# Retention attention and a low-rank mixer MLP on one core: the order of the start-up transfers, of the first batch's chunks, and of the work beside the first MLP

## The chip, the core and the metric

The kernel runs on one core of one Trainium2 chip. The metric is the device time of one execution in microseconds (us); a median of several executions stands for a kernel. The engines are PE (matmul; PEld is its weight load), DVE (vector), ACT (scalar), POOL (GpSimd) and SP (which only issues transfers). DMA engines move data between memory and the chip; a transfer is issued by SP, ACT or POOL, in the order of that engine's own program.

## The reference

Eight batches of 576 positions, 8 heads of 64. The attention is a decayed causal product without softmax, its output is the input x of a mixer along positions (rank 32), and that feeds an MLP of 512 to 2048 to 512:

```python
scores = scale * q @ k.T                      # per batch and head, 576 x 576
ret = scores * Dmat                           # Dmat[i, j] = gamma_h ** (i - j) for i >= j, else 0
x = (ret @ v)                                 # all heads side by side: 8 x 576 x 512
u = x + ((x.T @ U) @ V).T                     # U 576 x 32, V 32 x 576
out = u + relu(u @ w_ch1) @ w_ch2             # w_ch1 512 x 2048, w_ch2 2048 x 512, float32
```

## The kernel before

**Tiling.** Positions go in chunks of 128. Two batches p share one odd chunk: an even batch has four full chunks and the first half (64 rows) of chunk XC, an odd batch has the other half of XC and four more. A batch g is `Front(g)` and then `Mlp(g)`. Front computes the attention chunk by chunk in a recurrent form, and the mixer; Mlp is a phase Y1 (`u @ w_ch1`, relu; 16 feature blocks f) and a phase Y2 (`@ w_ch2`, 16 matmuls over f for each chunk of output).

**Front, per chunk c.** `TK` transposes k (for the first two batches on PE through a PSUM tile of the pool ps_big, which has three buffers; for later ones by a DMA that SP issues), `TQ` the queries, `TX` the q and k of chunk XC. `ST` (L425) adds k-times-v to a running state and ACT copies it out (L430). `SC` makes the scores (L446), then the product of the queries with the state of the chunk before, into tile po (L462), and DVE masks the scores (L471). `RV` multiplies the masked scores with v (L483), and DVE scales the result into x (L491). `MA` and `MH` are the mixer (L512, L529; DVE adds x at L535), `MT` (L548) transposes u into uT, the input of Y1 (L647). po and the scores' tile have one buffer each, so a chunk waits for DVE's reading of the chunk before.

**Loads and casts.** `load_q` (L253), `load_kv` (L284) and `load_x` (L305) are issued by SP as float32 into staging tiles: one buffer for q, four for k and v, one for x. `cast_q` and `cast_kv` turn them into bfloat16: DVE casts q and k, POOL scales v (`scale_v`, L274). `load_mixer` (L192 to L197) brings U and V in small pieces, six transfers for part 0 and five for part 1, on SP's queue. `load_w1` (L229) and `load_w2` (L239) are four transfers each, issued by POOL, which cast to bfloat16 on the way.

**The order.** It is all written out by hand (`tc.manual_schedule`): each engine runs its instructions strictly in the order in which the Python code emits them. A list of (time, function) pairs, sorted by time, lays Front's items between those of the MLP; the times are planned costs in ns, not waits. At the start:

- SP issues q and chunk 0 of batch 0, part 0 of the mixer, chunks 1 to 3, x, part 1 of the mixer.
- `early_consts` makes the decay tables (16 small DVE multiplications at L166, two ACT exponentials) and `first_front` runs batch 0's attention in the order 0, 1, 2, 3, XC, with 28 dummy matmuls (L697) between.
- POOL issues all of w1 ahead of chunk XC's work and, by the insertion after the fourth Y1 item, all of w2. Nothing is ahead of w2 in POOL's queue that has to wait, so its four transfers leave right behind w1's.
- `load_q(1)`, and with it the rest of batch 1 behind it in SP's queue, waits for the third w1 transfer (`return dmas[-2]`). `load_q(2)` waits for the last w2 transfer.
- `interleave(y1, fill, 0.75, 1.8)` lays the mixer's end of batch 0 and all of `Front(1)` beside and behind Y1 of batch 0; Y2 of batch 0 follows when Front(1) is over, three chunks abreast and then the fourth.
- From batch 1 on the list of timed events runs: Front(2) from 0.1 of Mlp(1), each later Front(g) up to 0.65 of Mlp(g-1).

```python
i = load_q(1)
tc.add_manual_dep(i.ins, w1_last.ins.name, SYNC)
...
y1.insert(4, (0, lambda: w2_last.append(load_w2())))
interleave(y1, fill, LEAD[0], LEAD[1])
lo2 = loads_of(2)
i = lo2.pop(0)[0]()
tc.add_manual_dep(i.ins, w2_last[0].ins.name, SYNC)
for f in range(NF):
    for i in range(3):
        mlp.Y2(i, f, 1)
```

Of the kernel before, what the change touches and what calls it, by code (L numbers as in the profile page):

```python
# [41 lines left out]
def kernel(  # L42
# [37 lines left out]
    LEAD = (0.75, 1.8)  # L80
# [40 lines left out]
    lnb = consts.tile([P, 1], FP32, name="lnb")  # L121
    U_A = consts.tile([P, 5, P], BF16, name="U_A")
# [19 lines left out]
    def early_consts():  # L142
        make_identity(nc, ident)
        nc.gpsimd.memset(lnb, math.log(scale))


        for t in (posk, posq):
            iota(t[:, XC, :], [[0, H]], 4 * P, 1)
            iota(t[HALF:P, XC, :], [[0, H]], -HALF, 1)
        iota(posk[:, 0:4, :], [[P, 4], [0, H]], 0, 1)  # L150
        iota(posk[:, 5:9, :], [[P, 4], [0, H]], 0, 1)
        for j in range(J):
            r = slice(j * PJ, (j + 1) * PJ)
# [10 lines left out]
        for h in range(H):  # L164
            for t in (posk, posq):
                nc.vector.tensor_scalar(  # L166
                    out=t[:, :, h], in0=t[:, :, h], scalar1=lng[h], scalar2=None,
                    op0=ALU.mult,
                )
# [3 lines left out]
    def clear_a():  # L173
        nc.vector.memset(ret_xa[HALF:P], 0.0)
# [13 lines left out]
    def load_mixer(par):  # L188
        f, t0, m0 = ((U_fA, 0, 0), (U_fB, HALF, 1))[par]
        src = moe_U[t0:t0 + 4 * P, :].rearrange("(m p j) r -> j p m r", p=PJ, j=J)  # L190
        for j in range(J):
            nc.sync.dma_start(out=f[j * PJ:(j + 1) * PJ, m0:m0 + 4, :], in_=src[j])  # L192
        if par == 0:
            nc.sync.dma_start(out=U_fA[0:HALF, 4, :], in_=moe_U[4 * P:S, :])
            nc.sync.dma_start(out=V_nat, in_=moe_V)
        else:
            nc.sync.dma_start(out=U_fB[HALF:P, 0, :], in_=moe_U[0:HALF, :])  # L197
# [26 lines left out]
    def load_w1():  # L224
        dmas = []
        for fb in range(dff // W1B):
            cols = slice(fb * W1B, (fb + 1) * W1B)
            dmas.append(
                nc.gpsimd.dma_start(  # L229
                    out=w1_sb[:, :, cols],  # L230
                    in_=moe_w_ch1[:, cols].rearrange("(c p) f -> p c f", p=P),
                )
            )
        return dmas[-2]

# [77 lines left out]
    def cast_x(p, part=None):  # L313
        f = sts[p]["x_f"]
        if part == 0:
            t = sts[p]["x3"]
        else:
            t = x3_pool.tile([P, 3, H, D], BF16, tag="x3", name="x3")
        rows = {None: slice(0, P), 0: slice(0, HALF), 1: slice(HALF, P)}[part]
        if part == 1:  # L320
            nc.vector.memset(t[0:HALF], 0.0)
        nc.vector.tensor_copy(out=t[rows, 0:2], in_=f[rows, 0:2])
        scale_v(t[:, 2], f[:, 2], XC, rows)
        sts[p]["qk", XC], sts[p]["v", XC] = t[:, 0:2], t[:, 2]
        sts[p]["k", XC] = t[:, 1]
        if part is None:
            nc.gpsimd.tensor_copy(out=vx[p % 2][HALF:P], in_=t[HALF:P, 2])
            sts[p]["vs", XC] = vx[p % 2]
        else:
            sts[p]["vs", XC] = t[:, 2]  # L330
# [5 lines left out]
    class Front:  # L336
# [96 lines left out]
        def SC(self, c, n=128, cross=True):  # L433
# [8 lines left out]
            psc = ps_sc.tile([P, 2, NHP, P], FP32, tag="ps_sc", name="psc")  # L442
            for hp in range(NHP):
                for hl in range(2):
# [4 lines left out]
                    )  # L449
            po = ps_o.tile([P, 2, 512], FP32, tag="ps_o", name="po")  # L450
            st["po", c] = po
            if c > 0 and cross:
                s_sb = st["s", c - 1]
# [5 lines left out]
                for hp in range(NHP):  # L459
                    for hl in range(2):  # L460
# [6 lines left out]
                        )  # L467
            ret = ret_xa if n < P else ret_pool.tile([P, H, P], BF16, tag="ret", name="ret")
# [35 lines left out]
        def MA(self, i, pool=None):  # L504
            st = self.st
            n = HALF if (self.quick and i == 4) else P
            if i == 0:
# [123 lines left out]
    class Mlp:  # L631
# [49 lines left out]

        def y2_items(self):
# [6 lines left out]
    def first_front():  # L689
# [16 lines left out]
        for c in range(5):  # L706
            if c < 4:
                fr.TK(c)
                if c < 3:
                    cast_kv(0, c + 1)  # L710
                else:
                    cast_x(0, 0)
                warm(WARM[1])
                fr.ST(c)
                if c:
                    fr.RV(c - 1)
                fr.SC(c)
            else:
                w1_last = load_w1()
                fr.TX(HALF)  # L720
                warm(WARM[2])
                fr.RV(3)
                fr.SC(XC, HALF)
            if c == 0:
                put_mixer_a()
            elif c > 1:
                fr.MA(c - 2)
            warm(WARM[3])
        fr.RV(XC, HALF, rows=slice(0, HALF))
# [15 lines left out]
        fr.MA(4)  # L745
        warm(WARM[4])
# [6 lines left out]
        warm(WARM[5])  # L753
        return fr, w1_last
# [24 lines left out]
    with tc.manual_schedule(engines={PE, POOL, SPQ, DVE, ACT}):  # L779
        load_q(0)  # L780
        for m in range(4):
            load_kv(0, m)
            if m == 0:
                load_mixer(0)
        load_x(0, 0)
        load_mixer(1)
        sts[0]["x3"] = x3_pool.tile([P, 3, H, D], BF16, tag="x3", name="x3")
        early_consts()
        clear_a()
        clear_b()  # L790
        first, w1_last = first_front()
        i = load_q(1)
# [5 lines left out]
        mlp = Mlp(0)  # L798
        fill = [(0, put_mixer_b)] + [(216, lambda c=c: first.MH(c)) for c in range(2)]
        fill += [(0, lambda: cast_kv(1, 0)), (0, lambda: cast_x(0, 1))]  # L800
        fill += [(0, lambda: cast_q(1, (0, 1))), (0, lambda: cast_q(1, (2, 3)))]
        fill += [(216, lambda c=c: first.MH(c)) for c in range(2, 4)]
        casts = [(lambda m=m: cast_kv(1, m),) for m in range(1, 4)]
        fill += Front(1, True).items(casts, x_alone=True)
        w2_last = []
        y1 = mlp.y1_items()
        y1.insert(4, (0, lambda: w2_last.append(load_w2())))
        interleave(y1, fill, LEAD[0], LEAD[1])
        lo2 = loads_of(2)
        i = lo2.pop(0)[0]()  # L810
        tc.add_manual_dep(i.ins, w2_last[0].ins.name, SYNC)
        for f in range(NF):
            for i in range(3):
                mlp.Y2(i, f, 1)
            if f % 3 == 1 and lo2:
                lo2.pop(0)[0]()
        mlp.Y2(3, 0, NF)
        for f in lo2:
            f[0]()


        main, starts = [], {}
        t = 0.0
        for g in range(1, NG):
            mlp = Mlp(g)
            starts[g] = t
            for c, f in mlp.y1_items() + mlp.y2_items():
                main.append((t, f))
                t += c
        starts[NG] = t  # L830
        events = list(main)
        lo = starts[1] + 0.1 * (starts[2] - starts[1])
        fronts = {g: Front(g, False) for g in range(2, NG)}
        for g in range(2, NG):
            hi = starts[g - 1] + SKEW * (starts[g] - starts[g - 1])
            items = fronts[g].items(loads_of(g + 1), nxt=fronts.get(g + 1))
            tot = sum(c for c, _ in items)
# [39 lines left out]
```

## Time and profile before

| what | value |
|---|---|
| median of 3 runs | 396.76 us (394.75 to 399.62) |
| the profiled execution | 395.17 us, of which the span (first to last instruction) 393.4 us |
| PE busy | 343.2 us (87%) |
| DVE, ACT, POOL busy | 153.3, 146.7, 54.5 us |
| moved by DMA | 49.67 MB |

Times in the rows are us from the start of the span unless a column says otherwise. PEclk is the granted clock of TensorE as a share of its full speed; a matmul row's second number is the time that the row's instructions took together. "[5.14 <-DVE o_sb]" is idle time of the engine just before the row and what ended it. POOLq and SPq are the queues' issues of transfers.

### The profile page before, as it was taken

How to read it: one execution, taken by the hardware profiler on the slowest of the kernel's cores; microseconds unless marked ns; L12 is line 12 of the kernel's file. 1: busy time of each engine (PE TensorE's matmuls, PEld its weight loads, DVE VectorE, ACT ScalarE, POOL GpSimd, SP SyncE). 2: the span in 40 equal slices, each digit the busy share in tenths (PEclk: the TensorE clock that was granted, in tenths of full speed). 3: DMA queues.
4: the chain of work that ended last, by engine and by line, in shares of the span. 5: the costliest groups of instructions: out<-in, count | busy, mean ns of one | idle time of the engine just before them, and what ended most of it. 6: DMA issues, size and time to landing. Idle time of an engine off the chain costs nothing.

```text
span 393.4 us, 6463 instructions
## 1 busy us (share of the span) xinstructions
PE 343.2 (87%) x2656; PEld 189.4 (48%) x2656; DVE 153.3 (39%) x246; ACT 146.7 (37%) x284; POOL 54.5 (14%) x83
## 2 busy tenths in 40 slices
PE   2889526789499999999799999997999999999991
PEld 1554213434266555454476554444665554557540
DVE  5752154651147355246341464355322551210020
ACT  2426315130156431651266314620664136328400
POOL 7370032410112120111202101111100000000000
PEclk9999958669879999999899999999899999999997
DMA  7979999919397944698999236989931210020122
GB/s 174 204 117 215 224 200 244 192 28 215 84 201 109 246 116 99 138 209 131 173 206 174 57 80 128 224 128 166 121 38 39 57 42 0 21 82 7 41 57 64
DMA packets 127246, 49.67 MB, mean 126 GB/s; under 512 B 110288, under 2 KB 122576, under 8 KB 127216
## 3 DMA queue, kind: packets, MB, share of 16 engines
q1 hardware_dynamic: 118192, 35.62, 53.1%
q10 hardware_dynamic: 4800, 9.44, 8.5%
q0 software_dynamic: 4224, 4.19, 6.5%
q8 instruction: 21, 0.34, 0.4%
q14 instruction: 9, 0.07, 0.1%
HBM read 36.92 MB, written 9.44 MB: 118 GB/s over the span
## 4 chain that ended last, share of the span: by engine, by line
PE 75%; DMA 7%; DVE 6%; SPq 4%; ACT 3%; issue 2%; POOL 1%; ACTq 0%; DVEq 0%; POOLq 0%
DMA kv_f<-in_v_dram 3%; PE po L483 3%; PE psc L446 3%; SPq L284 3%; PE psa L512 2%; DMA out_dram<-o_sb 2%; DVE ret L471 2%; PE pu L548 2%; PE ph L529 2%; PE pss L425 2%; DMA x_f<-in_q_dram 2%; SPq L305 1%; PE dummy L697 1%; PE po L462 1%; PE ps_y_3672 L657 1%
## 5 line engine op out<-in xcount | busy, mean ns | idle before, releaser
L647 PEld LDWEIGHTS <-w_sb 128*128 128x128 bf16 x768 | 74.3, 101 | 59.3 <-issue 11.5
L274 POOL TENSOR_TENSOR kv<-kv_f,vscale 128x512 bf16<-128x512 f32 x32 | 33.8, 1055 | 208.5 <-DMA kv_f<-in_v_dram 173.6
L471 DVE TENSOR_TENSOR ret<-psc,tri 128x1024 bf16<-128x1024 f32 x32 | 39.1, 1222 | 30.5 <-PE psc L446 30.5
L535 DVE TENSOR_TENSOR ut<-ph,xt 128x512 bf16<-128x512 f32 x36 | 24.5, 690 | 61.8 <-PE ph L529 61.8
L430 ACT ACTIVATE s_sb<-pss 128x512 bf16<-128x512 f32 x32 | 19.1, 597 | 57.9 <-PE pss L425 29.1
L491 DVE TENSOR_TENSOR xt<-po,qscale 128x512 bf16<-128x512 f32 (+1 forms) x37 | 25.5, 689 | 23.2 <-PE po L483 23.0
L348 ACT ACTIVATE uT<-pu 128x512 bf16<-128x512 bf16 x32 | 19.1, 596 | 23.8 <-PE pu L548 23.8
L483 PEld LDWEIGHTS <-ret 128*128 128x128 bf16 x288 | 13.3, 102 | 11.5 <-DVE ret L471 6.5
L370 PE MATMUL psq<-ident,q_bf 128*128 128x128 bf16 x32 | 4.0, 312 | 17.0 <-DVE q_bf L270 17.0
L294 DVE CAST kv<-kv_f 128x512 bf16<-128x512 f32 x32 | 14.1, 445 | 9.4 <-DMA kv_f<-in_k_dram 9.3
L483 PE MATMUL po<-kv,ret 128*128 128x64 bf16 x256 | 13.6, 199 | 3.4 <-DVE ret L471 3.2
L548 PEld LDWEIGHTS <-ut 128*128 128x128 bf16 x128 | 10.0, 102 | 9.2 <-DVE ut L535 3.0
L548 PE MATMUL pu<-ident,ut 128*128 128x128 bf16 x128 | 13.3, 230 | 0.7 <-DVE ut L535 0.7
L446 PE MATMUL psc<-qT,kT 64*128 64x128 bf16 x256 | 13.3, 226 | 0.0
L425 PEld LDWEIGHTS <-kv 128*128 128x128 bf16 x112 | 9.4, 106 | 6.4 <-issue 1.4
L446 PEld LDWEIGHTS <-kT 64*128 64x128 bf16 x256 | 7.6, 97 | 10.1 <-issue 9.2
L425 PE MATMUL pss<-kv 128*128 128x128 bf16 x112 | 11.9, 233 | 0.5 <-ACT s_sb L430 0.5
L657 PEld LDWEIGHTS <-y_4045 128*128 128x128 bf16 x80 | 7.8, 98 | 9.3
L370 PEld LDWEIGHTS <-q_bf 128*128 128x128 bf16 x32 | 3.2, 142 | 18.6 <-DVE q_bf L270 18.6
L270 DVE CAST q_bf<-q_f 128x512 bf16<-128x512 f32 x30 | 11.8, 455 | 0.0
L657 PEld LDWEIGHTS <-y_1108 128*128 128x128 bf16 x80 | 7.2, 98 | 7.7 <-issue 1.0
L697 PE MATMUL dummy<-ident 128*128 128x512 bf16 x28 | 9.5, 434 | 1.4 <-POOL ident masks.py:199 1.4
(579 smaller groups left out, 606.9 us busy)
## 6 DMA issues: line engine op xcount, KB each, us to landing
out_dram<-o_sb ACTq DMA_DIRECT2D x36, 256.0 KB
q_f<-in_q_dram SPq DMA_DIRECT2D x8, 1024.0 KB
kv_f<-in_k_dram SPq DMA_DIRECT2D x32, 256.0 KB
kv_f<-in_v_dram SPq DMA_DIRECT2D x32, 256.0 KB
w_sb<-in_moe_w_ch_dram POOLq DMA_DIRECT2D x8, 512.0 KB, 13.3
x_f<-in_k_dram SPq DMA_DIRECT2D x8, 128.0 KB
x_f<-in_q_dram SPq DMA_DIRECT2D x8, 128.0 KB
x_f<-in_v_dram SPq DMA_DIRECT2D x8, 128.0 KB
```

The source lines that it names most:

```text
L274: nc.gpsimd.tensor_tensor(out=dst[rows], in0=src[rows], in1=vscale[rows, c, :, None].to_broadcast([n, H, D]), op=ALU.mult,)
L348: nc.scalar.activation(out=dst, in_=src, func=AF.Copy)
L425: nc.tensor.matmul(pss[:, hp, :], pair_cols(st["k", c], hp), pair_cols(vt, hp), start=(first and hp == 0), stop=True, skip_group_check=True,)
L430: nc.scalar.activation(out=s_sb, in_=pss, func=AF.Copy)
L446: nc.tensor.matmul(psc[0:n, hl, hp, 0:n], kT[pb:pb + HALF, hp, 0:n], qTv[pb:pb + HALF, hp, 0:n], start=True, stop=True,)
L471: nc.vector.tensor_tensor(out=ret[0:n].rearrange("p (hp hl) i -> p hl hp i", hl=2)[:, :, :, 0:n], in0=psc[0:n, :, :, 0:n], in1=mask[0:n, N ...
L483: nc.tensor.matmul(po[0:n, hl, hp * D:(hp + 1) * D], ret[:, h, 0:n], vt[:, h, :], start=((c == 0 or not cross) and hp == 0), stop=True, sk ...
L491: nc.vector.tensor_tensor(out=st["x", c][rows].rearrange("p (hp hl d) -> p hl hp d", hl=2, d=D), in0=po[rows, :, 0:NHP * D].rearrange("p h ...
L535: nc.vector.tensor_tensor(out=ut, in0=ph, in1=st["x", c], op=ALU.add)
L548: nc.tensor.transpose(pu[:, cc, :], self.st["u", c][:, cc * P:(cc + 1) * P], ident)
L647: nc.tensor.matmul(ps[:, 0:n], w1_sb[:, cc, f * P:(f + 1) * P], uT[:, cc, t0:t0 + n], start=(cc == 0), stop=(cc == NCC - 1),)
L657: nc.tensor.matmul(self.ps[i], self.y1[:, f, i * P:(i + 1) * P], w2_sb[:, f, :], start=(f == 0), stop=(f == NF - 1),)
```

## The change

The order of transfers becomes batch 0, w1, batch 1, w2, batch 2, by where POOL and SP are made to wait:

- SP's queue holds at the start q, chunks 0, 1, 2, then x, then chunk 3. The mixer's pieces go to ACT's queue, part 0 at the start and part 1 behind the first front.
- POOL issues two transfers of w1 behind x's `scale_v` and two behind that of chunk 3. `load_q(1)` waits for the second of them. POOL then scales v of batch 1's chunks 0, 1 (and x between), 2, and only then issues w2, then scales chunk 3. `load_q(2)` waits for the second w2 transfer.
- The first front's order is 0, 1, 2, XC, 3. Scores of XC and 3 are taken apart from the product with the state (`CR`) and from the mask (`MK`). Fewer dummy matmuls (12 in place of 28). The decay tables take two DVE multiplications, and the clears on DVE stand ahead of them.
- Batch 0's MLP joins the list of timed events. Its Y2 is emitted two chunks abreast, f by f (`y2_by_f`). The rest of batch 0's mixer and Front(1) are spread over 0.47 to 0.9 of Mlp(0), which by planned costs is from the end of Y1 through most of Y2. Batch 2's loads and casts are spread from 0.75 of Mlp(0) to 0.12 of Mlp(1). Front(2) begins at 0.15 of Mlp(1).

```diff
-    LEAD = (0.75, 1.8)
+    FILL1 = (0.47, 0.9)
+    LOAD2 = (0.75, 0.12)
+    FRONT2 = 0.15
...
     def load_mixer(par):
-            nc.sync.dma_start(out=f[j * PJ:(j + 1) * PJ, m0:m0 + 4, :], in_=src[j])
+            nc.scalar.dma_start(out=f[j * PJ:(j + 1) * PJ, m0:m0 + 4, :], in_=src[j])
...
-        return dmas[-2]
+        return dmas[-1]
     def load_w2():
...
+        return dmas[1]
...
+        def y2_by_f(self):
+            return [
+                (216, lambda i=i, f=f, j=j: self.Y2(i + j, f, 1))
+                for i in range(0, self.nch, 2) for f in range(NF) for j in range(2)
+            ]
...
+        put_mixer_a()
+        cast_x(0, 0)
+        fr.SC(2)
...
+        fr.TX(HALF)
+        fr.RV(2)
+        fr.MA(1)
+        w1a = load_w1(range(0, 2))
+        cast_kv(0, 3)
+        w1b = load_w1(range(2, 4))
+        fr.SC(XC, HALF, None)
...
+        fr.SC(3, cross=None)
+        fr.CR(XC, HALF)
         fr.RV(XC, HALF, rows=slice(0, HALF))
...
+        load_mixer(1)
         i = load_q(1)
         tc.add_manual_dep(i.ins, w1_last.ins.name, SYNC)
         for m in range(4):
             load_kv(1, m)
             if m == 0:
                 load_x(0, 1)
+        for m in range(4):
+            cast_v(1, m)
+            if m == 0:
+                cast_xv(0, 1)
+            if m == 2:
+                w2_part = load_w2()
...
+        for g in range(NG):
+            for c, f in mlp.y1_items() + (mlp.y2_by_f() if g == 0 else mlp.y2_items()):
...
+        spread(fill, at(0, FILL1[0]), at(0, FILL1[1]))
...
+            tc.add_manual_dep(f().ins, w2_part.ins.name, SYNC)
...
+        spread(lo2, at(0, LOAD2[0]), at(1, LOAD2[1]))
+        lo = at(1, FRONT2)
```

## Rows read from the trace of the kernel before

**Rows 1.** The page's head and its span in 40 slices (9.8 us each)

```profile
span 393.4 us, 6463 instructions
...
PEclk9999958669879999999899999999899999999997
DMA  7979999919397944698999236989931210020122
```

**Rows 2.** Table by stretch: us; busy (instructions) of each engine, PEclk, DMA share, GB/s

```profile
8.00:10.00 2.00, 1.06 (x11) 1.06 (x12) 1.98 (x5) 1.27 (x4) 1.06 (x1) 1.00 0.26 56
10.00:20.00 10.00, 8.36 (x101) 5.51 (x100) 7.41 (x13) 4.61 (x7) 3.24 (x4) 1.00 1.30 204
44.40:56.00 11.60, 0.98 (x5) 0.25 (x3) 2.23 (x5) 0.60 (x1) 1.25 (x2) 0.63 1.24 199
56.00:85.20 29.20, 20.47 (x208) 12.16 (x209) 17.23 (x26) 11.57 (x18) 10.01 (x10) 0.68 0.80 170
106.30:112.00 5.70, 5.68 (x24) 3.29 (x24) 0.90 (x2) 1.90 (x5) 0.00 (x0) 0.50 0.90 146
112.00:393.40 281.40, 267.84 (x2075) 148.97 (x2072) 106.23 (x155) 112.52 (x227) 24.27 (x26) 0.98 0.60 108
```

**Rows 3.** PE's timeline, 31 to 112 us: start, us, instructions, idle before

```profile
31.16 1.03 PE L647 MATMUL ps_y_560<-uT,w_sb 128*128 128x512 bf16 x4
32.03 1.03 PE L647 MATMUL ps_y_566<-uT,w_sb 128*128 128x512 bf16 x4
...
56.08 0.61 PE L370 MATMUL psq<-ident,q_bf 128*128 128x128 bf16 x4 [10.70 <-DVE q_bf L270]
...
99.92 0.71 PE L647 MATMUL ps_y_1109<-uT,w_sb 128*128 128x320 bf16 x4
...
106.32 1.23 PE L647 MATMUL ps_y_1121<-uT,w_sb 128*128 128x320 bf16 x4 [5.14 <-DVE o_sb L665]
```

**Rows 4.** SP's queue, 0 to 80 us: start, us, transfer issued

```profile
3.56 4.15 SPq L192 DMA_DIRECT2D U_fA<-in_moe_U_dram  x4
...
8.98 0.42 SPq L284 DMA_DIRECT2D kv_f<-in_k_dram  x1
...
32.55 0.38 SPq L253 DMA_DIRECT2D q_f<-in_q_dram  x1
...
58.54 0.96 SPq L253 DMA_DIRECT2D q_f<-in_q_dram  x1
```

**Rows 5.** POOL's timeline, 0 to 80 us

```profile
20.81 1.03 POOL L274 TENSOR_TENSOR x_166<-x_f,vscale 64x512 bf16<-64x512 f32 x1 [1.23 <-DMA x_f<-in_v_dram]
21.80 3.17 POOL L229 DMA_DIRECT2D w_sb<-in_moe_w_ch_dram  x4
24.93 3.00 POOL L239 DMA_DIRECT2D w_sb<-in_moe_w_ch_dram  x4
53.10 1.04 POOL L274 TENSOR_TENSOR kv<-kv_f,vscale 128x512 bf16<-128x512 f32 x1 [25.18 <-DMA kv_f<-in_v_dram]
...
60.01 1.04 POOL L274 TENSOR_TENSOR kv<-kv_f,vscale 128x512 bf16<-128x512 f32 x1 [1.15 <-DMA kv_f<-in_v_dram]
```

**Rows 6.** The weights' tile: time from issue to landing of its eight transfers

```profile
DMA to landing us min/median/max: 5.5/13.3/24.0
```

**Rows 7.** Y2 of one chunk; chain of waits, 16 matmuls late in the span

```profile
343.90 3.45 PE ps_y_4005 L657 x16
```

**Rows 8.** Groups by shape on all engines, 56 to 86 us: busy, mean ns, idle before

```profile
L471 DVE TENSOR_TENSOR ret<-psc,tri 128x1024 bf16<-128x1024 f32 x4 | 4.9, 1220 | 0.8 <-PE psc L446 0.8
...
L491 DVE TENSOR_TENSOR xt<-po,qscale 128x512 bf16<-128x512 f32 x4 | 2.8, 692 | 2.1 <-PE po L483 2.1
...
L294 DVE CAST kv<-kv_f 128x512 bf16<-128x512 f32 x3 | 1.3, 419 | 0.0
```

**Rows 9.** Chain of waits, 56 to 112 us: start, us, what

```profile
96.45 9.00 DMA out_dram<-o_sb
...
109.68 1.07 PE ps_y_1139 L647 x4
```

More of the change, by code (lines that the diff above doesn't have):

```diff
@@ L163, in early_consts @@
         nc.gpsimd.memset(trix[0:HALF, HALF:P], 0.0)
[L164 to L169, printed above, removed]
+        for t in (posk, posq):
+            nc.vector.tensor_tensor(
+                out=t, in0=t, in1=lngs[:, None, :].to_broadcast([P, NCH, H]),
+                op=ALU.mult,
+            )
         nc.scalar.activation(out=vscale, in_=posk, func=AF.Exp, bias=lnb, scale=-1.0)
@@ L173, in clear_a @@
     def clear_a():
+        for h in range(H):
+            nc.vector.memset(lngs[:, h:h + 1], lng[h])
         nc.vector.memset(ret_xa[HALF:P], 0.0)
@@ L313, in cast_x, with x_rows, cast_xv, cast_xqk @@
     def cast_x(p, part=None):
[L314 to L319, printed above, removed]
+        cast_xv(p, part)
+        cast_xqk(p, part)
+    def x_rows(part):
+        return {None: slice(0, P), 0: slice(0, HALF), 1: slice(HALF, P)}[part]
+    def cast_xv(p, part=None):
+        st, f = sts[p], sts[p]["x_f"]
+        if part is None or part == 1:
+            st["x3"] = x3_pool.tile([P, 3, H, D], BF16, tag="x3", name="x3")
+        t = st["x3"]
         if part == 1:
-            nc.vector.memset(t[0:HALF], 0.0)
-        nc.vector.tensor_copy(out=t[rows, 0:2], in_=f[rows, 0:2])
+            nc.gpsimd.memset(t[0:HALF], 0.0)
+        rows = x_rows(part)
         scale_v(t[:, 2], f[:, 2], XC, rows)
-        sts[p]["qk", XC], sts[p]["v", XC] = t[:, 0:2], t[:, 2]
-        sts[p]["k", XC] = t[:, 1]
+        st["v", XC] = st["vs", XC] = t[:, 2]
+        st["qk", XC], st["k", XC] = t[:, 0:2], t[:, 1]
         if part is None:
             nc.gpsimd.tensor_copy(out=vx[p % 2][HALF:P], in_=t[HALF:P, 2])
-            sts[p]["vs", XC] = vx[p % 2]
-        else:
-            sts[p]["vs", XC] = t[:, 2]
+            st["vs", XC] = vx[p % 2]
+    def cast_xqk(p, part=None):
+        f, rows = sts[p]["x_f"], x_rows(part)
+        nc.vector.tensor_copy(out=sts[p]["x3"][rows, 0:2], in_=f[rows, 0:2])
     def pair_cols(t, hp):
@@ L449, in SC, with CR @@
                     )
+            if cross is not None:
+                self.CR(c, n, cross)
+            self.MK(c, n)
+        def CR(self, c, n=128, cross=True):
+            st = self.st
             po = ps_o.tile([P, 2, 512], FP32, tag="ps_o", name="po")
@@ L744, in first_front @@
                 )
-        fr.MA(4)
-        warm(WARM[4])
+        for c in range(3):
+            x_t(c, range(3))
+        fr.CR(3)
+        fr.RV(3)
+        fr.MA(4, 3)
+        for c in range(3):
+            x_t(c, range(3, 4))
+        fr.MA(3, 3)
+        x_t(3)
         for cc in range(NCC):
@@ L797, with spread @@
                 load_x(0, 1)
-        mlp = Mlp(0)
+        for m in range(4):
+            cast_v(1, m)
+            if m == 0:
+                cast_xv(0, 1)
+            if m == 2:
+                w2_part = load_w2()
         fill = [(0, put_mixer_b)] + [(216, lambda c=c: first.MH(c)) for c in range(2)]
-        fill += [(0, lambda: cast_kv(1, 0)), (0, lambda: cast_x(0, 1))]
+        fill += [(0, lambda: cast_k(1, 0)), (0, lambda: cast_xqk(0, 1))]
         fill += [(0, lambda: cast_q(1, (0, 1))), (0, lambda: cast_q(1, (2, 3)))]
         fill += [(216, lambda c=c: first.MH(c)) for c in range(2, 4)]
-        casts = [(lambda m=m: cast_kv(1, m),) for m in range(1, 4)]
+        casts = [(cast_k, 1, m) for m in range(1, 4)]
         fill += Front(1, True).items(casts, x_alone=True)
[L805 to L837, printed above, removed]
+        events, starts = [], {}
+        def spread(items, lo, hi):
+            tot = sum(c for c, _ in items) or len(items)
             at = 0.0
@@ L840, with at, first_load @@
                 events.append((lo + (hi - lo) * at / tot, f))
-                at += c
+                at += c if tot != len(items) else 1
+        t = 0.0
+        for g in range(NG):
+            mlp = Mlp(g)
+            starts[g] = t
+            for c, f in mlp.y1_items() + (mlp.y2_by_f() if g == 0 else mlp.y2_items()):
+                events.append((t, f))
+                t += c
+        starts[NG] = t
+        def at(g, share):
+            return starts[g] + share * (starts[g + 1] - starts[g])
+        spread(fill, at(0, FILL1[0]), at(0, FILL1[1]))
+        lo2 = [(0, f) for f, in loads_of(2)]
+        def first_load(f=lo2[0][1]):
+            tc.add_manual_dep(f().ins, w2_part.ins.name, SYNC)
+        lo2[0] = (0, first_load)
+        spread(lo2, at(0, LOAD2[0]), at(1, LOAD2[1]))
+        lo = at(1, FRONT2)
+        fronts = {g: Front(g, False) for g in range(2, NG)}
+        for g in range(2, NG):
+            hi = at(g - 1, SKEW)
+            spread(fronts[g].items(loads_of(g + 1), nxt=fronts.get(g + 1)), lo, hi)
             lo = hi
```

102 lines of the change are left out of this document (52 added, 50 removed).

## The prediction

> **What bounds the kernel now.** I read the page's head and slices first. The reader is to see two parts there: a long one with the clock at 9 and a short one, slices 6 to 12, where PEclk falls to 5 and 6 although the DMA digits stay at 9 up to the eighth slice, 79 us [rows 1]. The table by stretch says the same in numbers. From 112 us to the end PE is busy 267.8 of 281.4 us at clock 0.98: that part is matmul-bound, and nothing in the change makes its matmuls fewer. From 44.4 to 56 us PE is busy 0.98 of 11.6 us while the DMAs run at 199 GB/s; from 56 to 85.2 us it is busy 20.5 of 29.2 us at clock 0.68 [rows 2]. PE's timeline tells what is there: Y1 of batch 0 from 31.16 us, an idle 10.7 us until batch 1's queries have arrived and been cast, Front(1) with next to nothing beside it, then Y2 of batch 0, and Y1 of batch 1 from 99.92 us, with one more stall of 5.14 us in it [rows 3]. The queues' timelines show why batch 1 came so late: w1's four issues on POOL at 21.80 us, w2's right behind at 24.93 us, although w2 is first used after 85 us, and batch 1 on SP from 32.55 us, in company with w2 [rows 4, 5]. So the start is bound by the order of transfers, and then by a Front that runs alone.
>
> I cut the span in three: the moment X at which Y2 of batch 0 can begin; the time from X to the first Y1 of batch 1 (99.92 us before, [rows 3]); the rest.
>
> **First part: the transfers up to w2.** The mixer's six pieces leave SP's queue. Before, they were issued from 3.56 us on, and the next load of k went out at 8.98 us [rows 4]; from 8 to 10 us the DMAs moved 56 GB/s against 204 in the 10 us after [rows 2]. Filled at 204, those 2 us give 2 x (1 - 56/204) = 1.45 us. x now comes ahead of chunk 3's two loads of 262 KB, 0.52 MB / 204 = 2.57 us. POOL had x at 20.81 us [rows 5]; now 20.81 - 1.45 - 2.57 = 16.8, and behind its 1.03 us the first w1 issue is at 17.8 us (21.80 before).
>
> On ACT the six pieces stand where ACT has nothing to do. The Trainium skill, page "DMA: Bandwidth & Descriptors", section "Issuing engines are not separate DMA queues", says that transfers from several engines share the same 16 DMA engines, and that spreading them saves only the issuing engine's time. By that rule the 1.45 us would be lost again and the result 1.5 us later; the 56 GB/s speak for an issue that was the limit, so I keep the gain.
>
> The landing of a w transfer: at least 5.5 us after its issue [rows 6], which I give to the first, 21.8 + 5.5 = 27.3 us. The third had landed when SP went on at 32.55 us [rows 4]: two in 5.2, 2.6 us each. The last, issued near 27.1 us, took 24.0 [rows 5, 6], to 51.1: five in 18.5 us, 3.7 each in batch 1's company. So the gate of batch 1, now the second transfer, opens at 17.8 + 5.5 + 2.6 = 25.9 us.
>
> From gate to v of batch 1's chunk 2 on POOL took 60.01 - 32.55 = 27.5 us before [rows 4, 5], with five w transfers beside it; now two are, three fewer at 2.6: 19.7 us, so 45.6 us. As a cross-check, the 3.0 MB up to there take 14.8 us at 204 GB/s, and two transfers 5.2: 20.0. The added wait is on POOL: behind its three scalings of v and that of x stands w2. The last takes 1.04 us, w2 is issued at 46.6 and its first quarter lands 5.5 later: **X = 52.1 us**. Behind w2 only chunk 3's v waits on POOL, and that is needed later. Bounds of X: 47 us (w1's rest costs batch 1 nothing: 14.8 in place of 19.7) to 60 (the former 27.5 in place of 19.7).
>
> **What X covers.** Everything else in the first front, the new order, `CR` and `MK` apart, fewer dummies, the two multiplications in place of 16, the clears put forward, ACT's five pieces ahead of the first relu, moves only the start of Y1(0). That was 31.16 us; 16 items at 0.87 [rows 3] are 13.8 us, four MH under 1 us. Before X = 52.1 they need a start by 37.3 us. I take 28 us, bounds 25 (data 4 us earlier) and 36 (the five pieces at the 4.15 us of [rows 4]'s four, and a half-speed clock for want of dummies). All of it lies under the wait; without that cover each us late would be one us of time. PE idles some 9 us ahead of X.
>
> **Second part: X to the first Y1 of batch 1.** Y2(0) is four chunks at 3.45 us [rows 7], 13.8. Front(1) by the list's own costs is 10.06 us (TQ 0.90, four TK 0.92, TX 0.46, the XC items 0.77, then 0.93 + 0.69 + 2.08, MA 1.08, MH 1.08, MT 1.15); from above, the window's 20.47 busy x 0.68 clock = 13.9 less two Y1 items, 12.2 [rows 2]. I take 10.1. The clock: behind the 5.14 us stall PE ran from 106.3 to 112 us at 0.50 [rows 2], with 1.07 us for an item [rows 9] of 320 columns, which at full clock is 0.87 x 320/512 = 0.54 [rows 3], five of them: 2.6 us lost. The 9 us of idle ahead of X will cost that again. The chain inside Front: DVE needs 1.22 (mask) + 0.69 (x) + 0.42 (cast of k) = 2.33 us for a chunk [rows 8], PE with the Y2 matmuls between some 2.5, so DVE fits, but not always ahead. I count a full mask for XC, whose scores have no such company, one for the last chunk, and a quarter for each of the other four: 3 x 1.22 = 3.7, say 4; bounds 1 and 12. That includes the PSUM tiles: two of ps_big's three are held by the two chunks of Y2, and the transposes share the third.
>
> Sum: 52.1 + 13.8 + 10.1 + 2.6 + 4.0 = **82.6 us** for the first Y1 of batch 1, against 99.92.
>
> w2's other quarters land 2.6 us and then 3.7 us apart; Y2 with Front between takes four f in about 3.3 us, slower at first, so they are just in time. Batch 2: its gate, w2's second quarter, is at 54.7 us (58.54 before, [rows 4]); the transfers then ran for some 20.5 us, to 79 [rows 1], and now share with two quarters, 5.2: 80.4 us. Its last cast stands 2.7 us into Mlp(1), at 85.3. Cover 5 us; lost, it would stall DVE, whose next mask is then late.
>
> **Third part.** From 99.92 to the end were 393.4 - 99.9 = 293.5 us. The stall of 5.14 us was DVE's wait for a staging buffer of the output behind a store of 9.0 us [rows 3, 9]: four chunks ended together on three buffers. Two at a time, the first store leaves half a Y2, over 10 us, before the fourth needs its buffer; the stall goes, and the 2.6 us of half clock behind it. 293.5 - 5.1 - 2.6 = 285.8. Front(2)'s start at 0.15 in place of 0.1 I cost at nothing (bounds -1 and 3): its end at 0.65 stays, and PE is full there either way.
>
> Span 82.6 + 285.8 = 368.4; the profiled execution is 1.8 longer than its span, 370.2; the median stands at 396.76/395.17 = 1.004 of that execution: **372 us**, 6% faster.
>
> **The rivals.**
> - *Nothing is gained by the interleaving.* Front(1) stays bound by its chain from scores to mask to values, and Y2 beside it waits as well, since PE keeps the order. For it: the waits of PE for DVE in that window. Against: there were no matmuls to put between. Price: 29.2 us less 2.7 for two Y1 items, 26.4, in place of 10.1 + 2.6 + 4.0: 9.7 later, 382 us.
> - *X comes early and PE stays in step.* X at 47.2, one us of stalls, no clock loss: 4.9 + 3 + 2.6 = 10.5 us earlier, 361.5 us. For it: w1's second half would be mostly through before batch 1's first bytes flow, if a load is slow to start. Against: the 9 us of idle ahead of X.
> - *Batch 2 or the stores become the bound.* Transposes for Front(2) stand on SP behind batch 2's loads, and the load of batch 3's q with them. At 80.4 plus 5 for q and 5 for two pairs of transposes the first scores run at 90 instead of 87.7; with the store stall back, 7.7 more: 10 later, 382 us. Everything else would have to fail too for no change.
> - *Slower: w2 is late behind POOL's queue.* One engine in order: if v of chunk 2 comes late, w2 leaves late, and Y2, Front(1) and all behind it stand on PE. Each us of X is one us. Time is even at X = 393.4 - 285.8 - 30.5 = 77.1, with w2 issued at 71.6; 2% slower from X = 85, time 405. For it: X is on three serial landings. Against: chunk 2's v was on POOL at 60.01 us with a gate 6.7 us later and more company [rows 4, 5].
> - *The gates don't act:* w2 issued early after all. Not possible by POOL's order [rows 5].
>
> **How the numbers follow.** The forecast 0.55, serial Front 0.18, early X 0.17, batch 2 or stores 0.07, late w2 0.03. The forecast's own bounds (X, chain) are about 363 to 381. The early case lies at 361.5 and the two late ones at 382; going a little past each leaves 2 in 10 outside: 360 to 386. What a measurement can tell from no change is about 2%, 388.8 us. Faster by more than that: 0.55 + 0.17 + 0.21 of the late cases' 0.28, 0.93; the same 0.05; slower 0.02.
>
> **What would show it.** Right: the second w1 landing and SP's load of q near 26 us; POOL's w2 issues near 46.6; the first Y2 near 52 behind idle PE; its clock at 0.5 there for some 6 us; first Y1 of batch 1 near 83; no wait of o_sb for a store. Wrong: an X off by over 4 us, Front(1) over 25 us long from X on with PE waiting for masks, or a new PE stall behind Y1(1) that ends on batch 2's loads or transposes.

## The result, and the profile after

The changed kernel takes 375.41 us (median of 4 runs, 375.22 to 377.56), the kernel before 395.75 us in the same comparison; the ratio is 0.959, 95% interval 0.946 to 0.972. On another chip, with 6 and 17 runs, it was 374.17 against 390.54 us, 0.961 (0.956 to 0.967). The ratios here and below compare only executions in the undisturbed, fast state, the medians are of all executions, so the two do not always divide out. The forecast was 372 us, range 360 to 386.

The page's head and slices of the changed kernel, against [rows 1]:

```profile
span 373.8 us, 6393 instructions
...
PEclk9999699999996999999999999999999999999998
DMA  9989899959998876999998346999902200110112
```

The stretch of low clock, seven slices before, has become two single slices with a 6 (37 to 47 us, in Y1 of batch 0, and 112 to 121 us, in Front(2)). In the first fourteen slices the DMA digits fall below 8 only once, to 5; before there were a 1 and a 3 among them, and three 7s.

PE's timeline of the changed kernel, 28 to 114 us, against [rows 3]:

```profile
28.77 1.19 PE L676 MATMUL ps_y_555<-uT,w_sb 128*128 128x512 bf16 x4
...
38.84 1.87 PE L676 MATMUL ps_y_573<-uT,w_sb 128*128 128x512 bf16 x4 [7.15 <-ACT y_554 L680]
...
54.66 0.39 PE L686 MATMUL ps_y_678<-w_sb,y_554 128*128 128x512 bf16 x1 [0.33 <-DMA w_sb<-in_moe_w_ch_dram]
55.45 1.40 PE L387 MATMUL psq<-ident,q_bf 128*128 128x128 bf16 x16 [0.41 <-DVE q_bf L274]
...
88.23 0.71 PE L676 MATMUL ps_y_1082<-uT,w_sb 128*128 128x320 bf16 x4
...
112.28 0.40 PE L487 MATMUL po<-s_sb,qTx_131 64*128 64x64 bf16 x8 [4.05 <-POOL qTx_131 L481]
```

Read from below: the first Y1 of batch 1 comes at 88.23 us in place of 99.92. Front(1) and Y2 of batch 0 run together from X = 54.66 us, where Y2 waits last, by 0.33 us, for w2. Y1 of batch 0, which should have run through from 28.77 us, stands for 7.15 us on ACT, and Front(2) has a stall of 4.05 us that was not there before.

The same in stretches of the changed kernel (columns as in [rows 2]):

```profile
28.70:38.80 10.10, 2.91 (x12) 1.17 (x12) 0.93 (x4) 1.23 (x4) 0.00 (x0) 0.88 1.15 248
...
54.60:88.00 33.40, 26.74 (x257) 13.70 (x263) 20.51 (x33) 11.21 (x17) 5.90 (x6) 1.00 0.97 199
...
112.00:118.60 6.60, 6.10 (x36) 3.64 (x38) 0.69 (x1) 1.75 (x4) 1.27 (x2) 0.52 0.65 156
118.60:373.80 255.20, 243.60 (x1822) 134.20 (x1846) 94.89 (x137) 99.86 (x198) 20.85 (x22) 0.99 0.63 109
```

From 54.6 to 88 us PE is busy 26.7 of 33.4 us at full clock; before, Front(1) with two items of Y1 beside it had 20.5 of 29.2 at 0.68, and Y2 followed it.

POOL's timeline of the changed kernel, against [rows 5], then SP's, against [rows 4], then ACT's:

```profile
17.59 2.08 POOL L278 TENSOR_TENSOR x_162<-x_f,vscale 64x512 bf16<-64x512 f32 x1 [1.29 <-DMA x_f<-in_v_dram]
19.62 1.68 POOL L233 DMA_DIRECT2D w_sb<-in_moe_w_ch_dram  x2
...
47.85 1.04 POOL L278 TENSOR_TENSOR kv<-kv_f,vscale 128x512 bf16<-128x512 f32 x1 [1.29 <-DMA kv_f<-in_v_dram]
48.84 3.03 POOL L243 DMA_DIRECT2D w_sb<-in_moe_w_ch_dram  x4
```

```profile
4.75 0.37 SPq L288 DMA_DIRECT2D kv_f<-in_v_dram  x1
...
27.85 0.37 SPq L257 DMA_DIRECT2D q_f<-in_q_dram  x1
```

```profile
29.05 1.51 ACTq L196 DMA_DIRECT2D U_fB<-in_moe_U_dram  x3
37.66 0.49 ACTq L201 DMA_DIRECT2D U_fB<-in_moe_U_dram  x1
38.20 0.60 ACT L680 ACTIVATE y_554<-ps_y_555 128x512 bf16<-128x512 f32 x1 [8.87 <-DMA q_f<-in_q_dram]
```

The gates act as the diff says: batch 1 leaves at the second w1 landing, w2 behind chunk 2's v. ACT's lines explain the 7.15 us: the fifth of the mixer's small transfers could be issued only at 37.66 us, which the trace puts down to the landing of batch 1's queries, and the relu behind it in ACT's program waited that long.

### The profile page after: what moved, and what is told of

It reads as the page before. It is cut to its first block, busy times and chain, and to the rows that moved or that the text cites. A ratio compares the mean times of both kernels' runs of the same rounds, so it can differ in the third digit from the quotient of the medians.

```text
span 373.8 us, 6393 instructions
## 1 busy us (share of the span) xinstructions
PE 332.6 (89%) x2604; PEld 183.5 (49%) x2640; DVE 153.3 (41%) x239; ACT 146.2 (39%) x284; POOL 57.4 (15%) x84
## 4 chain that ended last, share of the span: by engine, by line
PE 74%; DMA 11%; DVE 5%; ACT 2%; SPq 2%; issue 2%; POOL 1%; ACTq 1%; POOLq 0%; DVEq 0%
DMA kv_f<-in_v_dram 4%; DVE ret L500 3%; DMA q_f<-in_q_dram 3%; PE psc L464 2%; PE po L512 2%; PE pu L577 2%; DMA w_sb<-in_moe_w_ch_dram 2%; PE ph L558 2%; PE psa L541 2%; DMA U_fA<-in_moe_U_dram 2%; PE pss L442 2%; DMA x_f<-in_v_dram 1%; PE ps_y_1679 L686 1%; PE ps_y_2028 L686 1%; PE ps_y_3702 L686 1%
## 5 line engine op out<-in xcount | busy, mean ns | idle before, releaser
L676 PEld LDWEIGHTS <-w_sb 128*128 128x128 bf16 x768 | 73.5, 99 | 59.2 <-issue 13.7
L306 DVE CAST kv<-kv_f 128x512 bf16<-128x512 f32 x32 | 15.4, 487 | 6.0 <-DMA kv_f<-in_k_dram 6.0
L464 PEld LDWEIGHTS <-kT 64*128 64x128 bf16 x256 | 7.4, 96 | 12.6 <-issue 10.1
L577 PE MATMUL pu<-ident,ut 128*128 128x128 bf16 x128 | 12.4, 219 | 0.8 <-DVE ut L564 0.4
L686 PEld LDWEIGHTS <-y_4025 128*128 128x128 bf16 x80 | 7.8, 98 | 9.3
L442 PEld LDWEIGHTS <-kv 128*128 128x128 bf16 x112 | 8.6, 100 | 5.6 <-issue 1.1
L686 PEld LDWEIGHTS <-y_1081 128*128 128x128 bf16 x80 | 7.1, 98 | 6.7
L686 PEld LDWEIGHTS <-y_2206 128*128 128x128 bf16 x80 | 7.2, 98 | 6.6
L686 PEld LDWEIGHTS <-y_3199 128*128 128x128 bf16 x80 | 7.2, 98 | 6.6
L686 PEld LDWEIGHTS <-y_3748 128*128 128x128 bf16 x64 | 6.1, 98 | 6.8
```

The costliest lines, as they stand in the source:

```text
L442: nc.tensor.matmul(pss[:, hp, :], pair_cols(st["k", c], hp), pair_cols(vt, hp), start=(first and hp == 0), stop=True, skip_group_check=True,)
L464: nc.tensor.matmul(psc[0:n, hl, hp, 0:n], kT[pb:pb + HALF, hp, 0:n], qTv[pb:pb + HALF, hp, 0:n], start=True, stop=True,)
L577: nc.tensor.transpose(pu[:, cc, :], self.st["u", c][:, cc * P:(cc + 1) * P], ident)
L676: nc.tensor.matmul(ps[:, 0:n], w1_sb[:, cc, f * P:(f + 1) * P], uT[:, cc, t0:t0 + n], start=(cc == 0), stop=(cc == NCC - 1),)
L686: nc.tensor.matmul(self.ps[i], self.y1[:, f, i * P:(i + 1) * P], w2_sb[:, f, :], start=(f == 0), stop=(f == NF - 1),)
```

## Experiments

Twelve runs in three groups (e1 to e4, e5 to e8, e9 to e12), each on a chip of its own; the runs of a group share the runs of the kernel before. The medians of the kernel before were 390.39, 393.99 and 390.54 us, so across groups the ratios compare better than the medians.

| run | what | median us | ratio to before (95%) |
|---|---|---|---|
| e1 | changed, Front(1) ahead of Y2 | 385.62 | 0.986 (0.980 to 0.992) |
| e2 | changed, mixer part 1 on SP, early | 376.39 | 0.962 (0.956 to 0.968) |
| e3 | e2, w2 right behind w1 | 376.74 | 0.963 (0.956 to 0.970) |
| e4 | e2, w2 behind chunk 0 and x | 375.13 | 0.955 (0.947 to 0.964) |
| e5 | before, Front(1) spread over Y2 | 380.96 | 0.972 (0.942 to 1.003) |
| e6 | e4, Front(2) from 0.25 | 374.44 | 0.962 (0.951 to 0.974) |
| e7 | e4, batch 1 without a gate | 373.03 | 0.959 (0.949 to 0.969) |
| e8 | e2, mixer part 0 on SP too | 378.14 | 0.971 (0.957 to 0.985) |
| e9 | before, Y2 of batch 0 in pairs | 389.79 | 1.000 (0.996 to 1.004) |
| e10 | e5 again | 382.91 | 0.983 (0.976 to 0.990) |
| e11 | changed, again | 374.17 | 0.961 (0.956 to 0.967) |
| e12 | e7, Front(1) spread to 0.98 | 375.40 | 0.961 (0.955 to 0.967) |

**e1: the spreading undone.**

```diff
-    FILL1 = (0.47, 0.9)
+    FILL1 = (0.47, 0.49)
```

> The changed kernel with FILL1 ending at 0.49 in place of 0.9: all of Front(1) is emitted ahead of Y2 of batch 0 again, transfers as changed. If laying Front(1) between the matmuls of Y2 is worth what the prediction says (Front's chain of some 26 us then stands alone, with Y2's 13.8 us behind it), the first Y1 of batch 1 comes near 94 us in place of 88.2, and the time is 379 to 384 us. If the order of transfers alone made the gain and PE waits as much either way, it stays at 374 to 377.

Measured: 385.62 us, some 10 us above the changed kernel, and 1.6 us above the range expected. PE's timeline of e1:

```profile
53.88 1.62 PE L387 MATMUL psq<-ident,q_bf 128*128 128x128 bf16 x16 [2.06 <-DVE q_bf L274]
...
94.69 5.83 PE L676 MATMUL ps_y<-uT,w_sb 128*128 128x320 bf16 x40
...
106.27 0.61 PE L464 MATMUL psc<-qT,kT 64*128 64x128 bf16 x8 [4.98 <-DMA kT<-kv]
```

Front(1) begins as early as in the changed kernel, but the first Y1 of batch 1 comes 6.5 us later, and a stall of 4.98 us on a DMA transpose follows in Front(2). Interleaving does pay; the rival that it gains nothing is out.

**e2: ACT freed of the mixer's part 1.**

```diff
     load_mixer(0)
+    load_mixer(1, nc.sync)
...
-    load_mixer(1)
     i = load_q(1)
```

> The changed kernel with part 1 of the mixer issued by SP behind batch 0's loads in place of by ACT behind the first front. Both theories expect Y1 of batch 0 to run through from about 28.8 to 42.6 us, without the 7.15 us in which ACT's last piece stood at the full queue and no relu was done. If the landing of w2's first quarter sets the start of Y2 (54.66 us in the changed kernel, with 0.33 us of wait for it), Y2 still begins at 53 to 55 and PE idles 10 us ahead of it; time 374 to 378, the upper end if half clock then costs 2.6. If ACT's stall set it, Y2 begins near 47 and the time is 367 to 370.

Measured: 376.39 us, as the changed kernel. PE's timeline of e2:

```profile
52.64 0.61 PE L686 MATMUL ps_y<-w_sb,y 128*128 128x512 bf16 x1 [7.34 <-DMA w_sb<-in_moe_w_ch_dram]
```

and POOL's and SP's:

```profile
45.91 1.04 POOL L278 TENSOR_TENSOR kv<-kv_f,vscale 128x512 bf16<-128x512 f32 x1 [1.32 <-DMA kv_f<-in_v_dram]
46.90 3.37 POOL L243 DMA_DIRECT2D w_sb<-in_moe_w_ch_dram  x4
```

```profile
27.19 0.38 SPq L257 DMA_DIRECT2D q_f<-in_q_dram  x1
```

The 7.15 us on ACT have become 7.34 us on w2: most of the stall lay under the wait for w2. X came 2.0 us earlier than in the changed kernel (1.5 earlier than in e11, its second profile), which the total does not show. What held the issue on ACT, a full queue as the expectation has it or something else, no run shows. From 46.5 to 52.6 us PE is not busy at all and its clock is 0.50; here the half clock stands behind X, as the prediction had it.

**e3: w2 without its gate**, on e2.

```diff
     w1b = load_w1(range(2, 4))
+    w2_box.append(load_w2())
...
-        if m == 2:
-            w2_part = load_w2()
```

> The kernel of e2 with w2 issued right behind w1 (its own gate taken away; that of batch 1 stays at w1's second transfer). Theory of the prediction: six w transfers stand beside batch 1 in place of two, so batch 1 comes 6 to 8 us later (chunk 2's v on POOL at 53 to 56 us in place of 47.85); Front(1) is late by that much although w2 has landed; time 6 to 8 us over that of e2. Rival: what matters is only that Front(1) is spread over Y2, and w2 being early frees Y2; time as e2 or below.

Measured: 376.74 us, as e2; the theory of the prediction expected 6 to 8 us more. POOL's timeline of e3, then PE's:

```profile
23.60 2.98 POOL L243 DMA_DIRECT2D w_sb<-in_moe_w_ch_dram  x4
50.40 1.04 POOL L278 TENSOR_TENSOR kv<-kv_f,vscale 128x512 bf16<-128x512 f32 x1 [23.81 <-DMA kv_f<-in_v_dram]
...
57.57 1.19 POOL L278 TENSOR_TENSOR kv<-kv_f,vscale 128x512 bf16<-128x512 f32 x1 [1.52 <-DMA kv_f<-in_v_dram]
```

```profile
45.61 0.38 PE L686 MATMUL ps_y<-w_sb,y 128*128 128x512 bf16 x1
54.54 1.46 PE L387 MATMUL psq<-ident,q_bf 128*128 128x128 bf16 x12 [8.55 <-DVE q_bf L274]
```

Chunk 2's v did come 11.7 us later than in e2 (57.57 against 45.91), more than expected. But Y2 need not wait for w2 any more, and Front(1) begins at 54.54 in place of 53.04: in e2 batch 1 comes first and w2 is waited for, here it is the other way round. The stage needs both, and whichever comes last, Front(1) begins within 1.5 us of the same time.

**e4: w2 earlier**, on e2.

```diff
-        if m == 2:
+        if m == 0:
             w2_part = load_w2()
```

> The kernel of e2 with w2 issued behind the scaling of batch 1's chunk 0 and of x in place of behind chunk 2, some 5 us earlier. If each us of w2's landing is one us of time, Y2 begins near 49 to 50 and the time is 3 to 5 us below e2. If batch 1's chunks 1 to 3, which then share with w2, become late by as much and Front(1) waits for them, it is within 1 us of e2.

Measured: 375.13 us (371.22 to 377.16), 1.3 below e2, which the runs don't tell apart. PE's timeline of e4:

```profile
51.07 0.61 PE L686 MATMUL ps_y<-w_sb,y 128*128 128x512 bf16 x1 [5.73 <-DMA w_sb<-in_moe_w_ch_dram]
```

Issued 3.8 us earlier (43.08 against 46.90), w2 landed only 1.6 earlier; batch 1's rest then moved beside it, which is the likely reason. The first Y1 of batch 1 moved by 1.1 us (85.69 against 86.81). So most of what X gains arrives at the first Y1 of batch 1, but a us of issue is not a us of X.

**e5 and e10: the spreading alone**, on the kernel before, with its transfers, gates and first front. It takes in Y2 two chunks abreast, the spread casts of batch 2 and `FRONT2 = 0.15`.

```diff
-    interleave(y1, fill, LEAD[0], LEAD[1])
...
+    w2_part = load_w2()
+    spread(fill, at(0, FILL1[0]), at(0, FILL1[1]))
...
+    spread(lo2, at(0, LOAD2[0]), at(1, LOAD2[1]))
```

> The kernel before (its order and gates of transfers, its first front, its mixer on SP's queue), with one part of the change: batch 0's MLP in the timed list, Y2 two chunks abreast with Front(1) spread over it, batch 2's casts spread likewise. If the spreading is the larger part, Front(1) and Y2 start at 55 to 57 us as Front(1) did before, take some 34 us together as in the changed kernel, and the first Y1 of batch 1 comes at 89 to 92: 376 to 381 us, at least two thirds of the gain. If it is the order of the transfers that pays, 386 us or more.

> The kernel of e5 again (the kernel before with Front(1) spread over Y2, all transfers as before), beside the changed kernel on the same chip and in more rounds. From e1, e3 and e5: 377 to 381 us, 3 to 5 us above the changed kernel, and clearly below the kernel before. If the order of transfers were half of the gain, 384 us or more.

Measured: 380.96 us with a spread that decided nothing, then 382.91 us with ratio 0.983, clearly below the kernel before and clearly above the changed one (374.17 in the same group). So the spreading is half of the gain, where e5's theory had two thirds, and the time is 2 us above what I had narrowed it to. PE's timeline of e10, and one of PE's waits in it:

```profile
56.28 0.61 PE L372 MATMUL psq<-ident,q_bf 128*128 128x128 bf16 x4 [7.21 <-DVE q_bf L272]
...
91.37 5.83 PE L649 MATMUL ps_y<-uT,w_sb 128*128 128x320 bf16 x40
```

```profile
PE po L464 <- POOL qTx L458: 3.7, 1, 3.7
```

The old transfers bring Front(1) to a start at 56.28 us; in e11, the changed kernel on the same chip, it is 55.38. The spreading takes 7.6 of the 16.4 us by itself. Of the 8.7 us that the rest of the change adds to it, 0.9 lie in that start, 2.3 more up to the first Y1 of batch 1 (91.37 against 88.15), and 5.5 behind it (289.4 us to the end of the span against 284.0). The last number is not firm: in e5, the same kernel as e10, these were 285.2 us (from 92.86 us to the end of the span), and in the changed kernel's first profile 285.6. Two things came with the spreading and without the new transfers: in e5 and e10 too DVE waits for no store, and PE stands on POOL's copy in Front(2), 3.3 and 3.7 us, as in the changed kernel.

**e6: Front(2) later**, on e4.

```diff
-    FRONT2 = 0.15
+    FRONT2 = 0.25
```

> The kernel of e4 with Front(2) begun at 0.25 of Mlp(1) in place of 0.15. In e4 PE stood 2.2 us on the copy of chunk XC's queries, POOL's in turn on batch 3's v (in the changed kernel 4.0 us, and 6.8 us of half clock behind it). If Front(2) is only early, the stall goes and the time is 1 to 4 us below e4. If batch 3's loads follow Front(2)'s own casts and simply come later with it, the time is within 1 us of e4.

Measured: 374.44 us, within 1 us of e4. PE's wait for the copy of XC's queries is gone from its waits. The profiled execution reached the first Y1 of batch 1 2.4 us later than e4's (88.08 against 85.69), so its total doesn't price the stall that went. Behind that point it was no shorter (284.9 us to the end against 283.7), and PE stood 2.5 us there on ACT's copy of uT; what the stall costs stays open.

**e7: batch 1 without its gate**, on e4.

```diff
     i = load_q(1)
-    tc.add_manual_dep(i.ins, w1_last.ins.name, SYNC)
```

> The kernel of e4 without the gate of batch 1: its loads leave as soon as batch 0's have, beside w1. If what counts is only the sum of bytes up to w2 and the gap in DMA work ahead of w1's first bytes (131 to 150 GB/s in the third slice of these kernels), Y2 and Front(1) start 1 to 3 us earlier and the time falls by as much. If w1 late is worse, Y1 of batch 0 stalls on it (start at 32 to 36 us in place of 28.8), ends behind the landing of w2, and the time is 0 to 5 us above e4.

Measured: 373.03 us, lowest of all, but not told apart from e4 or from the changed kernel. SP issued the queries at 19.62 us in place of 27.13, and chunk 0's v was no earlier on POOL (40.71 us; 39.66 in e4). X was 51.86 us (51.07). Neither the gain nor the loss came: batch 1 left 7.5 us earlier, beside w1, and arrived no earlier.

**e8: part 0 of the mixer on SP too**, on e2.

```diff
     load_kv(0, m)
+    if m == 0:
+        load_mixer(0, nc.sync)
```

> The kernel of e2 with part 0 of the mixer on SP's queue too, behind chunk 0, as before the change. The prediction: w1's first issue 1.5 us later than the 18.1 us of e2, w2 and Y2 as much, time 1 to 2 us above e2. If the small pieces cost the same DMA time from either queue (in the changed kernel SP's load of v stood until 4.75 us behind them), w1's issue moves by less than 0.5 us and the time is within 1 us of e2.

Measured: 378.14 us, 1.7 above e2, though the two ran in different groups and their intervals overlap. POOL's timeline of e8, and the scaling of x in that of e2:

```profile
18.20 1.80 POOL L278 TENSOR_TENSOR x<-x_f,vscale 64x512 bf16<-64x512 f32 x1 [1.35 <-DMA x_f<-in_v_dram]
19.95 1.68 POOL L233 DMA_DIRECT2D w_sb<-in_moe_w_ch_dram  x2
```

```profile
17.10 1.04 POOL L278 TENSOR_TENSOR x<-x_f,vscale 64x512 bf16<-64x512 f32 x1 [1.19 <-DMA x_f<-in_v_dram]
```

x was there 1.1 us later than in e2, where the prediction said 1.45. w1's first issue is 1.9 us later (19.95 against 18.08), but 0.8 of that is a longer scaling of x, which the changed kernel also has in one of its two profiles and not in the other (2.08 and 1.03 us). w2's issue is 0.9 later and X 1.2 (53.80 against 52.64).

**e9: the pairs alone**, on the kernel before.

```diff
-    for f in range(NF):
-        for i in range(3):
-            mlp.Y2(i, f, 1)
...
-    mlp.Y2(3, 0, NF)
+    for i in (0, 2):
+        for f in range(NF):
+            for j in range(2):
+                mlp.Y2(i + j, f, 1)
```

> The kernel before with one edit: Y2 of batch 0 runs two chunks abreast and then the other two, behind Front(1) as before, in place of three and then the fourth. If the stall of 5.14 us at the first Y1 of batch 1 came from four outputs ending together on three staging buffers, the first store leaves some 7 us earlier, DVE's wait for it and the half clock behind it go, and the time falls by 5 to 8 us. If the stores are slow for another reason (they share the DMAs with batch 3's loads and transposes), the wait only moves and the time falls by less than 2 us.

Measured: 389.79 us, ratio 1.000 with an interval of 0.4% either way. ACT's timeline of e9 and its chain of waits:

```profile
93.51 11.22 ACTq L672 DMA_DIRECT2D out_dram<-o_sb  x3
104.77 1.09 ACT L651 ACTIVATE y<-ps_y 128x320 bf16<-128x320 f32 x3 [18.08 <-DMA out_dram<-o_sb]
```

```profile
94.42 0.02 SPq L385
94.44 0.03 issue
94.47 9.63 DMA kT<-kv
104.11 0.02 issue
104.12 0.02 ACTq L672
```

DVE no longer waits for a staging buffer, but ACT stands in its own queue: three stores took 11.22 us to issue, and by the chain what released the last was SP's DMA transpose of k, 9.63 us under way. The wait moved from DVE to ACT, and PE still stood 3.01 us on a relu.

**e11** is the measure of its group.

> The changed kernel, unedited, as the measure for the other runs on this chip: 374.5 to 377 us.

Measured: 374.17 us, 0.3 below the range given.

**e12: a wider spread**, on e7.

```diff
-    FILL1 = (0.47, 0.9)
+    FILL1 = (0.47, 0.98)
```

> The kernel of e7 with Front(1) spread up to 0.98 of Mlp(0) in place of 0.9, so that more of Y2's matmuls lie between Front's steps and 0.5 us of them behind it. If PE's short waits for DVE and ACT inside Front(1) (some 7 us from 54.6 to 88 us in the changed kernel) are filled by it, the time is 1 to 3 us below e7's 373.0 us. If Y1 of batch 1 then waits for the last uT, or the waits stay as they are, it is within 1 us of e7 or above.

Measured: 375.40 us, not below e7 and not told apart from e11. So nothing speaks for the short waits coming from a want of matmuls to put between.

## Why the prediction was right, and where its steps were not

The time was 3.4 us from the forecast, and the path is the one that was told: X, then Front(1) and Y2 together, then the rest. Against X = 52.1, 82.6 and a rest of 285.8 us stand 54.66, 88.23 and 285.6. The middle term was 33.6 us, and I had 30.5. The path held; that the sum came as close as it did is in part luck, as the terms below show.

**The transfers up to w2** were right to 2.6 us in the changed kernel, and in e2 nearly step by step: gate 25.9 (27.19 measured), chunk 2's v 45.6 (45.91), w2's issue 46.6 (46.90), X 52.1 (52.64). The changed kernel is later by the mixer's part 1 beside batch 1 and by a scaling of x that took 2.08 us in this one execution (1.03 in [rows 5], and 1.03 in e11, the same kernel again, with w2's issue at 48.26 us).

**"Behind w2 only chunk 3's v waits on POOL", and what the gates are worth.** The arithmetic of X held, but the reading that the order of transfers is what bounds the start did not. e3 took w2's gate away, e7 that of batch 1, and the time stayed. By the prediction's own working the gates only choose which of batch 1 and w2 comes last, and the interleaved stage needs both. No run of the changed kernel went without both; but e10 and e5, with the old order and the old gates, begin Front(1) at 56.28 and 57.39 us, only 1 to 2 us behind the changed kernel (55.45 and, in e11, 55.38).

**"What X covers"** held in the sum and failed in a term: I had ACT's five pieces at 4.15 us at most. The fifth was issued 8.6 us after the previous group began (37.66 against 29.05 us), Y1 ended at 52 us in place of 42, and the cover of some 9 us was used up: to within 0.33 us in the first profile, and wholly in e11, whose Y2 begins without a wait for w2:

```profile
54.16 0.39 PE L686 MATMUL ps_y<-w_sb,y 128*128 128x512 bf16 x1
```

There it was the late end of Y1 that set X, by a path that the prediction did not have. By e2 this cost 1.5 to 2 us of X and nothing that can be measured in the time.

**The half clock of 2.6 us behind X** did not come in the changed kernel: the clock is 1.00 from 54.6 to 88 us. PE had idled in Y1 instead, and the half clock fell there, ahead of X (0.86 from 38.8 to 54.6 us). In e2, with the idle where I had it, the clock was 0.94 from X on.

**The 4 us of waits inside Front(1) and Front's 10.1 us** are the terms that were mis-sized. PE was busy 26.7 us where 13.8 + 10.1 = 23.9 were counted, and idle for 6.7 where 4 were. The matmuls of Front take longer than its own list of costs says (the window's upper bound was 12.2, and with Y2 at its 13.8 even that was short by 0.7 us). Busy time was 2.8 us over and idle time 2.7; the 2.6 us of half clock that did not come took half of that back, which is luck. Where the waits are, PE's group rows of the changed kernel tell, 54.6 to 88.2 us:

```profile
L512 PE MATMUL po<-kv,ret 128*128 128x64 bf16 x32 | 1.6, 194 | 1.8 <-DVE ret L500 1.8
...
L512 PE MATMUL po<-x_541,ret 128*128 128x64 bf16 x8 | 0.4, 194 | 0.8 <-DVE ret L500 0.8
L464 PE MATMUL psc<-xT 64*128 64x128 bf16 x8 | 0.4, 219 | 0.7 <-ACT xT L365 0.7
```

The masks cost 1.8 + 0.8 = 2.6 us, where I had 3.7, with a quarter mask too many (Front(1) has XC and four chunks, so three others and not four); the rest are ten small waits, most of them on ACT's copies, DVE's casts and sums, which I had not counted one by one. One sign named for being wrong did come: Front(1) ran for some 30 us from X on (its last copy on ACT began at 85.63 us), over the 25 named. But PE waited only 2.6 us of that for masks, and a forecast stage of 30.5 us with Front(1) spread over it hardly left it less, so the sign was badly set.

**The rest of 285.8 us** was right only in its sum, and that is luck. The 293.5 us that it starts from belong to an execution of 395.17 us, longer than all 17 of the kernel before on the other chip (386.11 to 394.69). Over the changed kernel and its variants e2 to e4, e6 to e8, e11 and e12 the rest was 283.7 to 288.2 us. The wait of DVE for a store is gone from the changed kernel, but not for the reason given: e9 shows that two abreast alone only moves it to ACT, behind SP's transposes. e5 and e10 show that it goes with Front(1) beside Y2, under the old transfers too. How is a reading: with Front(1) beside Y2 the first store left at 74.57 us, before the first transpose at 83.98. In its place came the 4.05 us in Front(2), with a clock of 0.52 for 6.6 us behind, and by e5 and e10 that too comes with the spreading. It is the rival "batch 2 or the stores become the bound", in part, through batch 3's v, which POOL waited for ahead of its copy. Two waits of PE for ACT in the steady part of the kernel before, 2.4 and 2.1 us, are one of 1.5 in the changed kernel; but e5 and e10, two executions of one kernel, have 1.5 and 3.8, so the change can't be credited with it.

**The rivals.** Serial Front: e1 says that interleaving is worth 10 us, so it fell. Early X did not come, with X at 54.66 us; e4 and e7 come nearest, at X = 51.1 and 51.9. Late w2 was never near its point.

**How the gain divides.** Spreading alone takes 7.6 us, and 10 us are lost when it alone is undone; the 4.98 us stall in Front(2) that e1 has may be the difference, which no run shows. The transfers, the first front and the mixer's queue make the rest, 6 to 9 us. Of these each gate, taken away by itself, is worth nothing that can be measured, and the mixer's part 0 on ACT at most some 1.7 (e8, with intervals that overlap). What remains, x ahead of chunk 3 with w1's first issue at 18 to 20 us in place of 21.80, the new first front and the earlier gate of batch 2, was not run by itself. The traces find 0.9 to 2 us of it at the start of Front(1) and some 2 to 3 up to the first Y1 of batch 1; where the rest lies stays open.

## What to carry to other kernels

When a stage needs two sets of data and the DMAs are busy until both are in, ordering one ahead of the other can move which of them is waited for and hardly the moment when the stage can run, as in e3; look for work that can share a stage, which here was half of the gain. An engine that computes and also issues transfers can stand at an issue with its computing behind it, 8.87 us on ACT here: put such issues where nothing urgent follows, or on an engine that computes nothing. Two executions of one kernel can differ by 4 us over a stretch of 285 us (e5 and e10), so a gain of that size is not read from one profile. And a wait that goes from one engine may only have moved to the queue of another: undo or do the one edit alone before crediting it.

## What was not expected of the hardware

- A transfer of 8 KB on ACT's queue was not issued until 37.66 us, while 1 MB of queries moved on SP's queue. The six pieces on ACT's queue at the start delayed SP too, whose load of v was issued at 4.75 us; with these pieces on SP it was 1.86 (before, e8). The Trainium skill, page "DMA: Bandwidth & Descriptors", section "Issuing engines are not separate DMA queues", says that another issuing engine saves only the issuing time; e8 agrees in part: with the pieces on ACT x was scaled 1.1 us earlier (17.10 us in e2 against 18.20 in e8).
- Three stores of 256 KB took 11.22 us to issue on ACT while a DMA transpose was under way for 9.63 us (e9).
- Batch 1 without its gate was issued 7.5 us earlier, and its chunk 0's v was scaled no earlier (40.71 us in e7, 39.66 in e4).
